# Softcap attention with a maxout feed-forward: two batches loaded as seven tokens per row, and the weights loaded in another order

## Chip, cores, metric

One core of a Trainium2 chip. The time is device microseconds of a whole execution; the profile's span is about 2 us shorter. The runs of one kernel in one call spread over 0.6 to 1.9% here, and a verdict (faster, same, slower by 2%) uses fast runs only, with a 95% interval.

## The reference, cut to what matters

```python
# q, k, v: (8 batches, 12 heads, 448 tokens, 64); cap = 30
scores = cap * tanh(q @ k.T / sqrt(64) / cap)
attn   = softmax(scores)                      # max, exp, sum, division
x      = (attn @ v) -> (8 * 448 tokens, 768)  # heads side by side
out    = maximum(x @ w1, x @ w2) @ w_out      # w1, w2: 768 x 1024, w_out: 1024 x 768
```

## The kernel before

It works through 48 pairs of heads, one an iteration, in groups of three: load q, k, v; cast to bf16; turn q and k (by PE in the first 12 pairs, by DMA later); scores; tanh and exp on ACT; the product with v, which also gives the sums of the softmax; copy to `U`. A group's sums are gathered, inverted, written to DRAM and read back spread over the partitions, and POOL multiplies `U` by them into `x`. The feed-forward matmuls of finished batches fill PE's gaps (`F(n)` takes n of them). As max(a, b) = max(a - b, 0) + b, it uses w1 - w2 and a premultiplied w2 @ w_out.

A tile of 448 tokens is three rows of 128 and 64 more. Before, partition p holds tokens 3p to 3p+2, and the last 64 tokens come separately:

```python
def load(g, what, n0=0, n1=L):            # cut
    nc.sync.dma_start(out=m[:, 2*n0 : 2*n1, :],
        in_=src[b, h0:h1, 0 : NJ*P, :].rearrange("h (p j) d -> p h (j d)", j=NJ))
    ...                                   # the last 64 tokens: one or two more

def transposes(i):                        # pairs 0 to 11
    for j in range(8):
        nc.tensor.transpose(ps[:, j*P : (j+1)*P], kqf[g % 2][:, n, j, :], ident)
    nc.vector.tensor_copy(..., ps)

def invert(g, n0=0, n1=G):
    nc.vector.reciprocal(t[:m, :], sums[g, n0][:m, :])
    nc.sync.dma_start(out=d[:m, :], in_=t[:m, :])          # rec_d <- rec_s
    for h in range(2):                                     # rec_b <- rec_d
        nc.sync.dma_start(out=rb[64*h : 64*h+64, ...], in_=flat[h:h+1].to_broadcast(...))

# in moe(b): the store of 128 tokens of the result, 384 KB
    rows = out[b0*S : b0*S + NJ*P, :].rearrange("(p j) n -> p j n", j=NJ)
    nc.sync.dma_start(out=rows[:, j, :], in_=osb)
```

The buffers in question: `U` (two of 10.5 KB per partition), `osb` (three, for results), and the first `x` buffer, which stages w1 in two halves before it holds an x.

## Time and profile before

| | before |
|---|---|
| time, median of 4 runs | 392.12 us (390.2 to 392.63) |
| PE, ACT, POOL, DVE busy | 92%, 75%, 51%, 42% |
| U copies of pairs 4, 10, 47 on DVE | 44.22, 89.27, 337.94 us |
| stores of 384 KB | 24, median 3.9 us from issue to landing |

I later follow the kernel by the start of each pair's U copy, which DVE does once an iteration (pairs are counted from 0). The last 52 us have no attention left, only feed-forward.

### The profile page before, as it was taken

To read this page: it belongs to the slowest core of one execution; us is meant where nothing else is said; L and a number is where in the kernel's file an instruction comes from. 1 tells how busy PE (TensorE), PEld (TensorE's weight loads), DVE (VectorE), ACT (ScalarE), POOL (GpSimd) and SP (SyncE) were. 2 spreads that over 40 slices of the span, in tenths; PEclk is the share of its full clock that TensorE was granted. 3 is DMA by queue.
4 is the path that set the end of the run, shared out by engine and by line. 5 is a ranking of instruction groups with operands and counts; after the bars stand their busy time and mean duration, and the time that the engine had idled before them with its cause. 6 is when DMAs were issued, how large, how long until landed. Compare 5 with 4: busy or idle time off the path is not lost.

```text
span 390.3 us, 5720 instructions
## 1 busy us (share of the span) xinstructions
PE 358.5 (92%) x2128; PEld 171.8 (44%) x2128; DVE 164.3 (42%) x248; ACT 292.4 (75%) x289; POOL 199.6 (51%) x254
## 2 busy tenths in 40 slices
PE   3468896999999999989998999999999999999995
PEld 1123443544444444434443445444444444455563
DVE  5332657774434533253325433352345333633421
ACT  2699995878899799978998899889998899400000
POOL 4272269674638374656657464729482733651000
PEclk9995998999999999999999999999999999999999
DMA  6998899786779768967989597969796751322022
GB/s 142 280 252 180 242 288 274 198 202 165 149 199 252 198 171 199 260 181 192 217 225 223 142 237 210 255 166 225 219 188 179 166 142 65 90 73 100 23 81 81
DMA packets 106596, 71.50 MB, mean 183 GB/s; under 512 B 61384, under 2 KB 99400, under 8 KB 106568
## 3 DMA queue, kind: packets, MB, share of 16 engines
q1 hardware_dynamic: 104616, 67.99, 67.6%
q0 software_dynamic: 1952, 3.15, 4.6%
q8 instruction: 16, 0.26, 0.3%
q14 instruction: 12, 0.10, 0.1%
HBM read 53.48 MB, written 11.18 MB: 166 GB/s over the span
## 4 chain that ended last, share of the span: by engine, by line
PE 54%; DMA 17%; ACT 7%; SPq 6%; POOL 6%; DVE 5%; issue 3%; POOLq 0%; DVEq 0%; ACTq 0%
PE mm L318 15%; PE mm L333 11%; PE mm L330 9%; PE pv L250 8%; DMA rec_d<-rec_s 7%; DMA rec_b<-rec_d 6%; POOL xT L305 6%; PE s L231 5%; ACT expo L238 3%; ACT tanh L232 3%; DMA vm<-in_v_dram 3%; PE pv L259 2%; SPq L112 2%; SPq L101 1%; DMA xT<-in_moe_w_dram 1%
## 5 line engine op out<-in xcount | busy, mean ns | idle before, releaser
L232 ACT ACTIVATE tanh<-s 128x896 bf16<-128x896 f32 x144 | 126.0, 909 | 36.2 <-PE s L231 35.9
L305 POOL TENSOR_TENSOR xT<-u,rec_b 64x448 bf16<-64x448 f32 x95 | 108.2, 1139 | 86.1 <-DMA rec_b<-rec_d 73.8
L238 ACT ACTIVATE expo<-tanh 128x1792 bf16<-128x1792 bf16 x96 | 144.9, 1510 | 3.0
L265 DVE COPY u<-pv 128x896 f32<-128x896 f32 x48 | 52.3, 1091 | 105.3 <-PE pv L259 80.6
L333 PE MATMUL mm<-wo_sb,gT 128*128 128x384 bf16 x448 | 88.8, 327 | 0.0
L318 PE MATMUL mm<-xT,wd_sb 128*128 128x448 bf16 x384 | 80.8, 353 | 3.3 <-POOL xT L305 1.7
L330 PE MATMUL mm<-wm_sb,xT 128*128 128x384 bf16 x336 | 68.0, 327 | 1.8 <-DVE osb L337 1.8
L250 PE MATMUL pv<-expo,vp 128*128 128x448 bf16 x288 | 66.3, 367 | 1.1 <-ACT expo L238 1.1
L333 PEld LDWEIGHTS <-gT 128*128 128x128 bf16 x448 | 41.9, 98 | 36.5 <-issue 10.8
L337 DVE COPY osb<-mm 128x384 f32<-128x384 f32 x56 | 31.0, 555 | 59.9 <-PE mm L333 54.9
L318 PEld LDWEIGHTS <-wd_sb 128*128 128x128 bf16 x384 | 35.4, 98 | 43.9 <-issue 14.5
L231 PE MATMUL s<-qkT 64*128 64x448 bf16 x288 | 46.0, 370 | 7.7 <-DVE qkT L210 5.2
L322 DVE TENSOR_SCALAR gT<-mm 128x448 bf16<-128x448 f32 x64 | 39.9, 623 | 29.6 <-PE mm L318 28.6
L330 PEld LDWEIGHTS <-xT 128*128 128x128 bf16 x336 | 31.7, 98 | 28.6 <-issue 8.7
L250 PEld LDWEIGHTS <-vp 128*128 128x128 bf16 x288 | 28.2, 101 | 29.1 <-issue 7.7
L132 POOL CAST kqf<-qm 128x1152 bf16<-128x1152 f32 x15 | 17.2, 1147 | 33.9 <-DMA qm<-in_q_dram 33.7
L235 ACT ACTIVATE tanh<-s 128x448 bf16<-128x448 f32 x48 | 26.0, 542 | 4.3 <-PE s L234 4.1
L124 POOL CAST vp<-vm 128x576 bf16<-128x576 f32 x30 | 19.9, 665 | 14.2 <-DMA vm<-in_v_dram 9.4
L132 POOL CAST kqf<-km 128x1152 bf16<-128x1152 f32 x15 | 17.2, 1147 | 12.7 <-DMA km<-in_k_dram 11.9
L231 PEld LDWEIGHTS <-qkT 64*128 64x128 bf16 x288 | 10.9, 96 | 22.8 <-issue 15.1
L209 PE MATMUL mm<-ident,kqf 128*128 128x128 bf16 x96 | 9.8, 248 | 11.5 <-DVE kqf L132 7.7
L186 PE MATMUL mm<-wo_sb,w2T 128*128 128x384 bf16 x96 | 18.7, 328 | 0.0
(44 smaller groups left out, 158.9 us busy)
## 6 DMA issues: line engine op xcount, KB each, us to landing
rec_b<-rec_d SPq DMA_DIRECT2D x30, 336.0 KB, 5.0
out_dram<-osb SPq DMA_DIRECT2D x24, 384.0 KB, 3.9
km<-in_k_dram SPq DMA_DIRECT2D x15, 576.0 KB, 7.0
qm<-in_q_dram SPq DMA_DIRECT2D x15, 576.0 KB, 4.5
vm<-in_v_dram SPq DMA_DIRECT2D x15, 576.0 KB, 4.4
xT<-in_moe_w_dram SPq DMA_DIRECT2D x6, 512.0 KB
wo_sb<-in_moe_w_out_dram POOLq DMA_DIRECT2D x4, 384.0 KB, 7.3
gT<-in_moe_w_dram POOLq DMA_DIRECT2D x6, 256.0 KB, 5.8
```

Source lines behind the costliest of these rows:

```text
L132: eng.tensor_copy(t[:, n0:n1, o : o + NJ, :].rearrange("p n j (h d) -> p n h j d", h=2), m[:, 2 * n0 : 2 * n1, :].rearrange("p (n h) (j d) ...
L231: nc.tensor.matmul(s[:, h, :S], t[r, j * P : (j + 1) * P], qTn[r, :])
L232: nc.scalar.activation(tanh[i][:, 2 * j : 2 * j + 2, :], s[:, :, :S], AF.Tanh, scale=scale / cap)
L238: nc.scalar.activation(expo[i][:, c0:c1, :], tanh[i][:, c0:c1, :], AF.Exp, scale=float(cap))
L250: nc.tensor.matmul(ps[:, h, :S], vp[g % 2][:, n, h, j, :], e[:, 2 * j + h, :], start=(j == 0), stop=False)
L265: nc.vector.tensor_copy(U[g][:, :, n, :], pvt[i][:, :, :S])
L305: eng.tensor_mul(xT[b // 2][r, hp, cs], U[g][r, h, n, :], rec[g, n0][r, n - n0, :])
L318: nc.tensor.matmul(ps[:, :S], wd_sb[:, c, f * P : (f + 1) * P], x[:, c, cs], start=(c == 0), stop=(c == KC - 1))
L322: nc.vector.tensor_relu(g[:, f, cs], ps[:, :S])
L330: nc.tensor.matmul(ps[:, : DM // 2], x[:, c, ts], wm_sb[:, c, hs], start=(c == 0), stop=False)
L333: nc.tensor.matmul(ps[:, : DM // 2], g[:, f, ts], wo_sb[:, f, hs], start=False, stop=(f == FC - 1))
L337: nc.vector.tensor_copy(osb[:, hs], ps[:, : DM // 2])
```

## The change

Intent: fewer and longer packets at the start (1792 B in place of 768 and 256 B), a start in which ACT doesn't wait, weights that are there in time, and no wait for late w1 slices. In the first two batches a partition takes seven consecutive tokens of one head (64 rows a head, two heads for 128 partitions). PE then turns blocks of 64 x 64, and a tile of results holds token 2j of every row in its upper half and token 2j+1 in its lower half, so the store scatters. Cut to the core:

```diff
+    R7 = S // 64
+    def rows(t, b, h0, h1):
+        return t[b, h0:h1, :, :].rearrange("h (r j) d -> (h r) (j d)", j=R7)
     def load(g, what, n0=0, n1=L):
+        if g < NT:                                      # k and q; v has four pieces of its own
+            nc.sync.dma_start(out=t[...], in_=rows(src, b, h0, h1).rearrange("(n p) c -> p n c", p=P))
+            return
     def transposes(i):
-        for j in range(8):
-            nc.tensor.transpose(ps[:, j * P : (j + 1) * P], kqf[g % 2][:, n, j, :], ident)
+        for c, to in todo:                              # 13 blocks
+            for a in range(2):
+                r = slice(64 * a, 64 * a + 64)
+                nc.tensor.transpose(ps[r, to : to + 64], x[r, c : c + D], ident[r, r])
+        nc.tensor.transpose(ps[:, NJ * P : Q0], x[:, NJ * P : Q0], ident)
     def load_w1(c):
-        nc.sync.dma_start(out=w1_in[c % 2], in_=...)
+        w1_in[c] = opool.tile([P, DF], f32, name="osb")
+        nc.sync.dma_start(out=w1_in[c], in_=...)
     def pv_out(i):
+            if g == 0:
+                U[g] = x1.bitcast(f32)...               # the later home of x
     # in moe(b):
-                nc.sync.dma_start(out=rows[:, j, :], in_=osb)
+                if wide: ...                            # later batches, as before
+                else:
+                    o = o.rearrange("(r j) n -> j r n", j=R7)
+                    nc.sync.dma_start(out=o[2 * j : 2 * j + 2, :, :], in_=osb)
     # order: all of w_out and w2 from POOL after the casts of q and k of group 1; w1 from
     # iteration 2; v of group 0 behind q and k of group 1; for groups 0 and 1 the reciprocal
     # early in the iteration and its spread issued by POOL
```

More of the change, by code (lines that the diff above doesn't have):

```diff
@@ L40 @@
     NJ = 3
+    NT = 4
+    R7 = S // 64
     scale = 1.0 / (D ** 0.5)
@@ L69, with flat @@
     qf = [t[:, :, 4:8, :] for t in kqf]
+    def flat(g):
+        return kqf[g % 2].rearrange("p n j c -> p n (j c)")
     ident = const.tile([P, P], bf16, name="ident")
@@ L89, in half, with raw_of @@
         return slice(0, 64) if b % 2 == 0 else slice(64, P)
+    def rows(t, b, h0, h1):
+        return t[b, h0:h1, :, :].rearrange("h (r j) d -> (h r) (j d)", j=R7)
+    def raw_of(g, what):
+        if (g, what) not in raw:
+            raw[g, what] = stage.tile([P, 2 * L * NJ * D + (2 * L if what == "q" else L) * D], f32, name=what + "r")
+        t = raw[g, what]
+        m = t[:, : 2 * L * NJ * D].rearrange("p (h c) -> p h c", c=NJ * D)
+        l = t[:, 2 * L * NJ * D :].rearrange("p (h d) -> p h d", d=D)
+        return t, m, l
     def load(g, what, n0=0, n1=L):
@@ L94, in load @@
         src = {"k": k, "q": q, "v": v}[what]
-        if (g, what) not in raw:
-            raw[g, what] = (
-                stage.tile([P, 2 * L, NJ * D], f32, name=what + "m"),
-                stage.tile([P, 2 * L if what == "q" else L, D], f32, name=what + "l"),
+        t, m, l = raw_of(g, what)
+        if g < NT and what == "v":
+            x = rows(src, b, h0, h1).rearrange("(h r) c -> r h c", r=64)
+            for a in range(2):
+                nc.sync.dma_start(
+                    out=m[64 * a : 64 * a + 64, 2 * n0 : 2 * n1, :], in_=x[:, :, NJ * D * a : NJ * D * (a + 1)]
+                )
+            for par in range(2):
+                nc.sync.dma_start(
+                    out=l[64 * par : 64 * par + 64, n0:n1, :], in_=x[:, par::2, 2 * NJ * D :]
+                )
+            return
+        if g < NT:
+            nc.sync.dma_start(
+                out=t[:, n0 * S : n1 * S].rearrange("p (n c) -> p n c", c=S),
+                in_=rows(src, b, h0, h1).rearrange("(n p) c -> p n c", p=P),
             )
-        m, l = raw[g, what]
+            return
         nc.sync.dma_start(
@@ L119, in cast @@
         b = g * L // NP
-        m, l = raw[g, what]
+        x, m, l = raw_of(g, what)
         if what == "v":
@@ L128, in cast @@
                 eng.tensor_copy(vl[g % 2][r, n0:n1, r], l[r, n0:n1, :])
+            return
+        if g < NT:
+            x = x[:, n0 * S : n1 * S].rearrange("p (n c) -> p n c", c=S)
+            if what == "q":
+                eng.tensor_copy(flat(g)[:, n0:n1, Q0 : Q0 + S], x)
+                return
+            eng.tensor_copy(flat(g)[:, n0:n1, : NJ * P], x[:, :, : NJ * P])
+            for par in range(2):
+                r = slice(64 * par, 64 * par + 64)
+                eng.tensor_copy(kf[g % 2][r, n0:n1, 3, r], x[r, :, NJ * P :])
             return
@@ L148 @@
     x1 = xpool.tile([P, NP, 2 * S], bf16, name="xT").rearrange("p n s -> p (n s)")
-    w1_in = [x1[:, 2 * DF * j : 2 * DF * (j + 1)].bitcast(f32) for j in range(2)]
+    w1_in = {}
     w2b = (
@@ L164, in load_w1 @@
     def load_w1(c):
-        nc.sync.dma_start(out=w1_in[c % 2], in_=moe_w1[c * P : (c + 1) * P, :])
+        w1_in[c] = opool.tile([P, DF], f32, name="osb")
+        nc.sync.dma_start(out=w1_in[c], in_=moe_w1[c * P : (c + 1) * P, :])
     def subtract(c):
-        nc.vector.tensor_sub(wd_sb[:, c, :], w1_in[c % 2], w2b[:, c, :])
+        nc.vector.tensor_sub(wd_sb[:, c, :], w1_in[c], w2b[:, c, :])
     w2T = {}
@@ L207, in transposes @@
         ps = mm_psum.tile([P, 512], f32, name="mm").bitcast(bf16)
-        for j in range(8):
-            nc.tensor.transpose(ps[:, j * P : (j + 1) * P], kqf[g % 2][:, n, j, :], ident)
-        nc.vector.tensor_copy(qkT_of(g)[:, n, :, :].rearrange("p j c -> p (j c)"), ps)
+        x = flat(g)[:, n, :]
+        todo = [(j * D, (j % 3) * P + (j // 3) * 64) for j in range(6)]
+        odd = i // NP % 2
+        todo += [(Q0 + j * D, Q0 + (64 * j if not odd else 0 if j == 6 else 64 + 64 * j)) for j in range(R7)]
+        for c, to in todo:
+            for a in range(2):
+                r = slice(64 * a, 64 * a + 64)
+                nc.tensor.transpose(ps[r, to : to + 64], x[r, c : c + D], ident[r, r])
+        nc.tensor.transpose(ps[:, NJ * P : Q0], x[:, NJ * P : Q0], ident)
+        nc.vector.tensor_copy(qkT_of(g)[:, n, :, :].rearrange("p j c -> p (j c)")[:, : Q0 + S], ps[:, : Q0 + S])
     def cross(g):
@@ L221, in qk @@
         t = qkT[g][:, n, :, :].rearrange("p j c -> p (j c)")
-        o = Q0 + 64 * (i // NP % 2)
+        o = Q0 + (64 * (i // NP % 2) if g >= NT else 0)
         qTn = t[:, o : o + S]
@@ L263, in pv_out @@
         if n == 0:
-            U[g] = upool.tile([P, 2, G, S], f32, name="u")
+            if g == 0:
+                U[g] = x1.bitcast(f32).rearrange("p (h n s) -> p h n s", h=2, n=G)
+            else:
+                U[g] = upool.tile([P, 2, G, S], f32, name="u")
         nc.vector.tensor_copy(U[g][:, :, n, :], pvt[i][:, :, :S])
@@ L278, in gather @@
             )
+    recd = {}
     def invert(g, n0=0, n1=G):
@@ L283, in invert, with spread @@
         nc.vector.reciprocal(t[:m, :], sums[g, n0][:m, :])
-        d = dram.tile([16 * G, 56], f32, name="rec_d")
+        d = recd[g, n0] = dram.tile([16 * G, 56], f32, name="rec_d")
         nc.sync.dma_start(out=d[:m, :], in_=t[:m, :])
+    def spread(g, n0=0, n1=G):
         rb = rec[g, n0] = xpool.tile([P, G, S], f32, name="rec_b")
-        flat = d[:m, :].rearrange("(h n a) c -> h n (a c)", h=2, a=8)
+        lines = recd[g, n0][: 16 * (n1 - n0), :].rearrange("(h n a) c -> h n (a c)", h=2, a=8)
+        eng = nc.gpsimd if g < 2 else nc.sync
         for h in range(2):
-            nc.sync.dma_start(
+            eng.dma_start(
                 out=rb[64 * h : 64 * h + 64, : n1 - n0, :],
-                in_=flat[h : h + 1, :, :].to_broadcast([64, n1 - n0, S]),
+                in_=lines[h : h + 1, :, :].to_broadcast([64, n1 - n0, S]),
             )
@@ L323, in moe @@
         for t in range(3) if b % 2 == 0 else range(3, 7):
-            osb = opool.tile([P, DM], f32, name="osb")
+            osb = opool.tile([P, DF], f32, name="osb")[:, :DM]
             ts = slice(t * P, (t + 1) * P)
@@ L337, in moe @@
                 nc.vector.tensor_copy(osb[:, hs], ps[:, : DM // 2])
+            wide = b * NP >= NT * L
             if t == 3:
                 for n in range(2):
-                    r0 = (b - 1 + n) * S + NJ * P
-                    nc.sync.dma_start(out=out[r0 : r0 + 64, :], in_=osb[64 * n : 64 * n + 64, :])
-            else:
-                b0, j = (b, t) if t < 3 else (b, t - 4)
-                rows = out[b0 * S : b0 * S + NJ * P, :].rearrange("(p j) n -> p j n", j=NJ)
-                nc.sync.dma_start(out=rows[:, j, :], in_=osb)
+                    o = out[(b - 1 + n) * S : (b + n) * S, :]
+                    to = o[NJ * P : S, :] if wide else o.rearrange("(r j) n -> r j n", j=R7)[:, R7 - 1, :]
+                    nc.sync.dma_start(out=to, in_=osb[64 * n : 64 * n + 64, :])
+            else:
+                j = t if t < 3 else t - 4
+                o = out[b * S : (b + 1) * S, :]
+                if wide:
+                    nc.sync.dma_start(out=o[: NJ * P, :].rearrange("(p j) n -> p j n", j=NJ)[:, j, :], in_=osb)
+                else:
+                    o = o.rearrange("(r j) n -> j r n", j=R7)
+                    nc.sync.dma_start(out=o[2 * j : 2 * j + 2, :, :], in_=osb)
     fill_q = []
@@ L358 @@
     NL = N // L
-    NT = 4
     todo = [[] for _ in range(N)]
@@ L365 @@
     for g in range(2, NL):
-        e = 0 if g < NT else 2
-        at(3 * g - 6 - e, load, g, "k")
-        at(3 * g - 5 - e, load, g, "q")
-        at(3 * g - 4, load, g, "v")
-        at(3 * g - (5 if e else 4), cast, nc.gpsimd, g, "k")
-        at(3 * g - (5 if e else 3), cast, nc.gpsimd, g, "q")
-        at(3 * g - 2, cast, nc.gpsimd, g, "v")
-        if g >= NT:
-            at(3 * g - 4, cross, g)
-    at(1, cast, nc.gpsimd, 1, "v")
-    at(0, load_wo, 6)
-    for c in range(KC):
-        at(1 + c, load_w2, c)
-        at(2 + c, load_w1, c)
+        if g < NT:
+            e = 0 if g == 2 else 1
+            at(3 * g - 6 + e, load, g, "k")
+            at(3 * g - 6 + e, load, g, "q")
+            at(3 * g - 5 + e, load, g, "v")
+            at(3 * g - 4, cast, nc.gpsimd, g, "k")
+            at(3 * g - 4, cast, nc.gpsimd, g, "q")
+            at(3 * g - 3, cast, nc.gpsimd, g, "v")
+        else:
+            at(3 * g - 8, load, g, "k")
+            at(3 * g - 7, load, g, "q")
+            at(3 * g - 4, load, g, "v")
+            at(3 * g - 5, cast, nc.gpsimd, g, "k")
+            at(3 * g - 5, cast, nc.gpsimd, g, "q")
+            at(3 * g - 2, cast, nc.gpsimd, g, "v")
+            at(3 * g - 4, cross, g)
+    for c, i in enumerate((2, 2, 3, 4, 5, 6)):
+        todo[i].insert(c if i == 2 else 0, (load_w1, (c,)))
     MS = 3
     fill_const(nc.vector, 0)
-    fill_const(nc.gpsimd, 1)
-    load_wo(0)
-    for n0, n1 in ((0, 1), (1, L)):
-        for what in "kqv":
-            load(0, what, n0, n1)
-    for what in "kqv":
-        load(1, what)
-    for what in "kq":
-        cast(nc.vector, 0, what, 0, 1)
+    load(0, "k", 0, 1)
+    load(0, "q", 0, 1)
+    load(0, "k", 1, L)
+    load(0, "q", 1, L)
+    load(0, "v", 0, 1)
+    load(1, "k")
+    load(1, "q")
+    load(0, "v", 1, L)
+    load(1, "v")
+    cast(nc.vector, 0, "k", 0, 1)
+    cast(nc.gpsimd, 0, "q", 0, 1)
+    fill_const(nc.gpsimd, 1)
     transposes(0)
-    cast(nc.vector, 0, "v", 0, 1)
-    for what in "kqv":
-        cast(nc.vector, 0, what, 1, L)
+    cast(nc.vector, 0, "k", 1, L)
+    cast(nc.vector, 0, "q", 1, L)
     qk(0, 0)
@@ L398 @@
     ex(0, 0, 4)
+    transposes(1)
     qk(0, 2)
@@ L401 @@
     ex(0, 4, 7)
+    cast(nc.vector, 0, "v")
     cast(nc.gpsimd, 1, "k")
-    load_wo(2)
     cast(nc.gpsimd, 1, "q")
-    load_wo(4)
-    transposes(1)
+    for f in range(0, FC, 2):
+        load_wo(f)
+    for c in range(KC):
+        load_w2(c)
+    cast(nc.gpsimd, 1, "v")
     qk(1, 0)
@@ L435 @@
         F(4 if late else 8)
+        first = i < 2 * G + 2
+        if first and i >= G and n == 0:
+            invert(g - 1)
         if i + 1 < N:
@@ L440 @@
             f(*a)
+        if i == G + 1:
+            spread(0)
+        if i == G + 2 or i == 2 * G + 1:
+            normalize(i // G - 1)
         F(6)
@@ L444 @@
         F(6)
+        if i == 2 * G:
+            spread(1)
         if i == N - 1:
             invert(g, 0, G - 1)
-        elif i >= G and n == 0:
+            spread(g, 0, G - 1)
+        elif not first and n == 0:
             invert(g - 1)
-        if i >= G and n == 1:
+            spread(g - 1)
+        if not first and n == 1:
             normalize(g - 1)
@@ L458 @@
     invert(N // G - 1, G - 1, G)
+    spread(N // G - 1, G - 1, G)
     normalize(N // G - 1, 0, G - 1)
```

## The prediction

> **What bounds the kernel now.** I first read the busy time by stretch of the span, because the shares of the whole span (PE 92%, ACT 75%) are averages over stages with different limits. The rows, with PE, PEld, DVE, ACT and POOL busy, the granted clock, the DMA share and the rate:
>
> ```profile
> 0.00:10.00 10.00, 3.12 (x15) 1.16 (x15) 5.29 (x17) 3.12 (x4) 4.38 (x15) 1.00 0.64 147
> 10.00:20.00 10.00, 5.25 (x21) 1.69 (x22) 3.53 (x11) 6.98 (x7) 2.89 (x5) 1.00 1.09 280
> 20.00:30.00 10.00, 6.75 (x44) 3.02 (x41) 3.57 (x4) 9.78 (x11) 7.29 (x13) 0.94 1.14 246
> 30.00:40.00 10.00, 9.09 (x48) 3.66 (x45) 3.60 (x5) 9.87 (x11) 2.45 (x4) 0.54 0.84 175
> ...
> 60.00:70.00 10.00, 7.34 (x47) 3.65 (x47) 8.09 (x10) 5.47 (x7) 9.54 (x14) 0.83 0.86 231
> 70.00:80.00 10.00, 8.93 (x74) 4.87 (x73) 6.85 (x9) 8.00 (x8) 6.59 (x7) 1.00 0.77 200
> ...
> 100.00:120.00 20.00, 20.00 (x124) 9.70 (x122) 6.63 (x10) 18.42 (x19) 9.75 (x14) 1.00 0.89 215
> ```
>
> There are four stages. Until about 20 us the inputs arrive and ACT has gaps. From 20 to 60 us ACT is full (9.3 to 9.9 of 10): tanh and exp of one pair of heads take 3 x 0.909 + 0.542 + 1.697 + 1.323 = 6.3 us by the means of the costliest groups. From 60 to about 90 us nothing is full, with a hole at 60 to 70. After 100 us PE is full nearly to the end. So the change, which edits only the first 85 us or so, can save no more than what PE and ACT lose there; the 300 us behind are a fixed amount of PE work that only starts earlier.
>
> Next the timeline of those stages, with the idle time before an instruction in brackets. Startup, on ACT:
>
> ```profile
> 8.13 1.73 ACT L232 ACTIVATE tanh<-s 128x896 bf16<-128x896 f32 x2 [6.10 <-PE s L231]
> 17.14 1.73 ACT L232 ACTIVATE tanh<-s 128x896 bf16<-128x896 f32 x2 [2.96 <-PE s L231]
> ```
>
> The second hole is pair 1: its scores need the copy of its turned q and k, which DVE makes only after the casts of v, and those wait for v (cast at 14.68). The hole at 60 us:
>
> ```profile
> 52.95 0.59 SPq L165 DMA_DIRECT2D xT<-in_moe_w_dram  x1
> 58.73 2.10 DVE L168 TENSOR_TENSOR wd_sb<-xT,gT 128x1024 bf16<-128x1024 f32 x1 [2.97 <-DMA xT<-in_moe_w_dram]
> 62.35 0.61 PE L209 MATMUL mm<-ident,kqf 128*128 128x128 bf16 x8 [3.13 <-DVE wm_sb L191]
> 64.91 1.73 ACT L232 ACTIVATE tanh<-s 128x896 bf16<-128x896 f32 x2 [4.25 <-PE s L231]
> ```
>
> The third slice of w1 was issued at 52.95 us (its buffer is one of two, and SP had stood waiting for the reciprocals), landed at 58.73, and held DVE, which held the copy that frees PE's accumulator, which held ACT. Last, the marks I measure iterations by, the first weighted-value matmul of pairs 4 and 10:
>
> ```profile
> 41.15 1.43 PE L250 MATMUL pv<-expo,vp 128*128 128x448 bf16 x6
> 87.64 1.30 PE L250 MATMUL pv<-expo,vp 128*128 128x448 bf16 x6
> ```
>
> Six iterations took 46.5 us, 7.7 us each. The stalled one (pair 6 to 7, 54.8 to 65.5) took 10.7, the neighbours 6.6 to 7.1. The chain of work that ended last runs there through a loop of premultiply matmuls, DVE copies, the transposes and DVE again, at some 7.0 us, above ACT's 6.3.
>
> **What the Trainium skill says.** (1) "TensorE: Matmul & The Clock Gate", section "Back-to-back issue gap": about 56 ns per isolated matmul of 128 columns, and an issue floor of about 25 ns at 64 and fewer. The trace agrees at 128: eight transposes take 0.61 us with a mean of 248 ns each, so (610 - 248) / 7 = 52 ns from start to start. It has none of 64 columns. (2) "TensorEngine Tiling (Array Packing)", section "Key Properties": a change of tiling mode drains the array. No number here isolates that. (3) "DMA: Bandwidth & Descriptors", "Specifications": transfers below 512 B lose rate, and the limit of the memory per core is about 358 GB/s. The page of before has 61,384 of 106,596 packets under 512 B, and no slice above 288 GB/s, which agrees in direction. (4) "TensorE: Matmul & The Clock Gate", Part 1: an idle window of about 3.4 us halves the clock. The trace fits: after the 3.13 us wait above, the granted clock of 60 to 70 us is 0.83.
>
> **The change part by part.**
>
> *Seven tokens per row, pairs 0 to 11.* A load of k or q of a group becomes 384 packets of 1792 B in place of 768 of 768 B and 384 of 256 B, and one issue in place of three or two, at about 0.6 us of SP each. Before the first v load, SP issues 4 loads where it issued 5, each twice to four times as useful. Queue 1 now spends 0.676 x 390.3 x 16 / 104,616 = 40 ns of an engine per packet; if some 15 ns of that are fixed (my estimate, not separable here), the 4 x 1536 packets removed are worth 4 x 1536 x 15 / 16 = 5.8 us of the queue, spread over 50 us. That is slack, not path, after 20 us, where ACT is full. v keeps its packets.
>
> In return PE turns each pair by 26 transposes of 64 columns and one of 128 in place of 8 of 128. Before: 8 x 52 = 0.42 us of pace. After, at a floor of 28 ns (a choice between the skill's 25 and half of 56): 26 x 28 + 52 = 0.78 us, and I add 0.15 for two changes of tiling. Extra: about 0.5 us a pair, and I would believe 0.3 to 1.2, because the loads of such small weights might not hide. For pairs 0 to 4 this lies under ACT. For pairs 5 to 11, turned in iterations 3 to 9, it lies in the loop of 7.0 us.
>
> *Order of the start.* The first tanh hardly moves: k lands as now (cast at 3.42), q is cast at the same time by POOL, but 27 cold transposes cost about 1 us more than 8. I leave it at 8.1 us. Pair 1's transposes now come before pair 0's last scores and before the casts of v, so the 2.96 us hole closes. But the matmul that follows in PE's order, the value product of pair 0, still needs all of v of group 0, and v now queues behind k and q of group 1. Bytes ahead of and with it: 15 blocks of 229 KB, 3.44 MB; at an estimated 320 GB/s from 2.2 us it lands near 13 us, the casts are done near 15, the product (2.9 us cold, from 17.33 to 20.24 now) near 18, and the third tanh of pair 1 starts at 18.4 in place of 20.66. Gain carried to pair 4: about 2.3 us, a ceiling too, as ACT's idle time from 8.1 to 60 us is only about 4 us.
>
> *w1 staged in three output buffers, with its first two slices asked for in iteration 2.* SP is no longer blocked by reciprocals there, since the spread of the first two groups is issued by POOL. The 2.97 us wait of DVE goes. *U of the first group in the later home of x* removes the wait of the third group's first U copy for the first normalize. That copy came at 60.76 and the normalize ended at about 58.5, so it alone is worth nothing now, but it would be the next wait behind w1. Together they bring the 10.7 us iteration to an ordinary 7.0, which is 3.7 us.
>
> *w_out and w2 in one go.* The same ten loads on POOL, from about 16 to 23 us (4 x 0.77 + 6 x 0.55 = 6.4 us of POOL), 6.3 MB read. Queue 0 was busy 4.6% of the span, 18 us of all engines, so in one piece they end near 40 us if the other queue takes half. The first w2 block is needed in iteration 3, at about 33 us. This is tight, and I count nothing for it.
>
> Sum: the start -2.3, the hole -3.7, the transposes in six iterations from pair 4 to 10, 6 x 0.5 = +3.0. Net -3.0, so 392.45 - 3.0 = 389.4 us. After pair 10 PE's work is the same as before.
>
> **The rivals.** *A: the small transposes overlap wholly, or the loop of 7.0 us had room for them.* For it: PE is 8.9 busy of 10 at 70 to 80 us, and the 52 ns pace shows that weight loads hide. Against it: the chain that ended last goes through these transposes and the copy behind them. It would keep the 3.0 us: 386 us; with fewer collisions of DVE and POOL 384. *B: the transposes cost over 1 us each, by drains and weight loads.* For it: nothing in the trace; against: the 64-row score matmuls run at 0.48 us for four, so tiles of half the rows do overlap. The loss of 6 to 8 us eats the gain: 392 to 394 us. *C: the one-go weights starve what is needed first* (w2 in iteration 3, group 2, v of group 0). For it: the DMA share is 0.84 to 1.14 from 10 to 60 us already. A new hole of 3 us takes the place of the old one: 392 to 393 us. *D: fewer packets speed up everything early.* ACT is full from 20 to 60 us, so this only lifts the start, which is counted.
>
> **Range and chances.** All losses that the change can reach are about 2.3 + 7 us (PE's idle time in pairs 4 to 10 beyond its work), so faster by over 2% (below 384.6) needs nearly all of them and free transposes; I give it 0.14. Slower by over 2% (above 400.3) needs B or C at more than twice what I think likely: 0.04. The rest is 0.82. Rivals A and B set the range, 384 to 394.
>
> **What would show it right or wrong.** The first value product of pair 4 should start near 39 us, pair 10 near 84.5; no iteration between should be over 8.5 us; the 64-column transposes should take 0.9 to 1.1 us a pair; the subtract should never wait for w1; the third tanh of pair 1 should start near 18.4. It is wrong if v of group 0 lands after 16 us, if PE waits for w2 or w_out, if a group of transposes exceeds 1.5 us, or if PE after 100 us is no longer full.

## The result, and the profile after

The changed kernel takes **421.73 us** (418.18 to 423.19, 4 runs) against 392.12 of before: ratio 1.0751, interval 1.067 to 1.0833. A ratio here is the mean time of one kernel's fast runs over that of the other's of the same rounds, so not quite the ratio of the medians. It is slower by 7.5%, and far outside the predicted range.

Where the time went is seen best by the start of each pair's U copy (us):

| pair | before | after | after - before |
|---|---|---|---|
| 4 | 44.22 | 41.98 | -2.2 |
| 6 | 60.76 | 55.93 | -4.8 |
| 7 | 68.45 | 67.48 | -1.0 |
| 10 | 89.27 | 89.21 | -0.1 |
| 14 | 116.61 | 116.55 | -0.1 |
| 16 | 130.28 | 139.10 | +8.8 |
| 18 | 144.09 | 160.85 | +16.8 |
| 24 | 186.09 | 216.68 | +30.6 |
| 47 | 337.94 | 368.78 | +30.8 |

The stages that the argument was about, up to pair 14, end even. The whole loss comes in jumps after pair 14 (pair 15 is 6.5 us late) and up to pair 24, and nothing is lost after. The chain of work that ended last, of the kernel after, from 100 to 170 us (start, length, what):

```profile
108.16 10.70 DMA rec_d<-rec_s
...
125.93 9.91 DMA vr<-in_v_dram
139.12 10.17 DMA rec_d<-rec_s
```

`rec_d` is the write of a group's reciprocals, 10.5 KB. It takes 10.7 us. The timeline of before, of the SP queue and of POOL:

```profile
107.82 0.55 SPq L345 DMA_DIRECT2D out_dram<-osb  x1
108.47 0.37 SPq L285 DMA_DIRECT2D rec_d<-rec_s  x1
112.55 1.12 SPq L289 DMA_DIRECT2D rec_b<-rec_d  x2
116.44 1.13 POOL L305 TENSOR_TENSOR xT<-u,rec_b 64x448 bf16<-64x448 f32 x1 [3.45 <-DMA rec_b<-rec_d]
```

And of after:

```profile
107.42 0.64 SPq L410 DMA_DIRECT2D out_dram<-osb  x1
108.16 0.82 SPq L341 DMA_DIRECT2D rec_d<-rec_s  x1
119.01 1.14 SPq L348 DMA_DIRECT2D rec_b<-rec_d  x2
123.03 1.12 POOL L364 TENSOR_TENSOR xT<-u,rec_b 64x448 bf16<-64x448 f32 x1 [10.37 <-DMA rec_b<-rec_d]
...
130.37 1.09 DVE L319 COPY u<-pv 128x896 f32<-128x896 f32 x1 [8.48 <-POOL xT L364]
```

Up to the first store the two run 0.1 to 0.4 us apart. Then SP issues the read-back 4.1 us after the write in the one and 10.9 us after it in the other, POOL starts its multiply 6.6 us later, and DVE, whose U buffer POOL must free, stands for 8.5 us. What the DMA engines did meanwhile shows in the busy time by stretch (the last two numbers are the DMA share and the rate). Before:

```profile
113.00:115.00 2.00, 2.00 (x15) 0.86 (x13) 0.56 (x1) 1.59 (x3) 0.00 (x0) 1.00 0.57 177
115.00:117.00 2.00, 2.00 (x14) 0.76 (x12) 0.39 (x1) 1.97 (x3) 0.56 (x1) 1.00 0.89 214
```

After:

```profile
113.00:115.00 2.00, 2.00 (x14) 0.91 (x13) 0.56 (x1) 1.59 (x3) 0.00 (x0) 1.00 0.13 52
115.00:117.00 2.00, 2.00 (x14) 0.78 (x12) 0.45 (x1) 1.97 (x2) 0.00 (x0) 1.00 0.13 52
```

0.13 of 16 engines is two engines, at a steady 52 GB/s; the share stays so from 111 to 118 us (0.09 to 0.14 in windows of 1 us). The store's output view, `o[2*j : 2*j+2, :, :]`, is 2 x 64 x 768: its first dimension is 2. At 52 GB/s its 384 KB (393,216 bytes) take 7.6 us, an estimate that fits these 7 us, against a median of 3.9 us from issue to landing for the stores of before.

The second finding is at 60 us, where the old hole had been. Timeline of after:

```profile
59.95 0.49 DVE L339 RECIPROCAL rec_s<-sums 48x56 f32<-48x56 f32 x1 [2.94 <-DMA sums<-u]
60.91 0.90 PE L259 MATMUL mm<-ident,kqf 64*64 64x64 bf16 x26 [2.57 <-DVE wm_sb L234]
63.96 1.73 ACT L283 ACTIVATE tanh<-s 128x896 bf16<-128x896 f32 x2 [4.17 <-PE s L282]
```

DVE no longer waits for w1. In this profile it waits 2.9 us for the sums of the second group, as the reciprocal now comes early in DVE's order, and PE and ACT wait behind it just as before.

### The profile page after: what moved, and what is told of

Same layout as the page of the kernel before. It is cut to its first block, busy times and chain, and to the rows that moved or that the text cites. A ratio compares the mean times of both kernels' runs of the same rounds, so it can differ in the third digit from the quotient of the medians.

```text
span 421.4 us, 6150 instructions
## 1 busy us (share of the span) xinstructions
PE 366.6 (87%) x2356; PEld 174.1 (41%) x2356; DVE 160.4 (38%) x241; ACT 292.8 (69%) x289; POOL 201.2 (48%) x256
## 4 chain that ended last, share of the span: by engine, by line
PE 51%; DMA 24%; ACT 9%; SPq 6%; POOL 4%; DVE 3%; issue 2%; POOLq 0%; DVEq 0%; ACTq 0%
PE mm L377 13%; PE mm L392 10%; DMA rec_d<-rec_s 9%; PE mm L389 8%; PE pv L301 8%; DMA vr<-in_v_dram 7%; ACT expo L289 5%; DMA rec_b<-rec_d 4%; PE s L282 4%; POOL xT L364 4%; ACT tanh L283 4%; PE mm L229 3%; DMA sums<-u 2%; PE pv L310 2%; SPq L142 2%
## 5 line engine op out<-in xcount | busy, mean ns | idle before, releaser
L364 POOL TENSOR_TENSOR xT<-u,rec_b 64x448 bf16<-64x448 f32 x89 | 101.3, 1138 | 93.9 <-DMA rec_b<-rec_d 90.1
L319 DVE COPY u<-pv 128x896 f32<-128x896 f32 x45 | 49.1, 1091 | 120.8 <-PE pv L310 72.9
L377 PE MATMUL mm<-xT,wd_sb 128*128 128x448 bf16 x384 | 84.8, 366 | 9.2 <-POOL xT L364 8.7
L301 PE MATMUL pv<-expo,vp 128*128 128x448 bf16 x288 | 67.7, 371 | 13.0 <-DVE u L319 8.1
L389 PE MATMUL mm<-wm_sb,xT 128*128 128x384 bf16 x336 | 69.0, 330 | 8.4 <-DVE osb L396 8.4
L377 PEld LDWEIGHTS <-wd_sb 128*128 128x128 bf16 x384 | 36.4, 100 | 52.5 <-issue 25.0
L301 PEld LDWEIGHTS <-vp 128*128 128x128 bf16 x288 | 28.3, 101 | 41.5 <-issue 16.1
L154 POOL CAST vp<-vr 128x576 bf16<-128x576 f32 x30 | 19.9, 662 | 29.3 <-DMA vr<-in_v_dram 25.4
L173 POOL CAST kqf<-qr 128x1152 bf16<-128x1152 f32 x12 | 13.8, 1146 | 23.6 <-DMA qr<-in_q_dram 23.5
L310 PE MATMUL pv<-expo,vl 64*128 64x448 bf16 x96 | 18.1, 373 | 0.0
L285 PE MATMUL s<-qkT 128*128 128x448 bf16 x48 | 17.3, 361 | 0.7 <-ACT tanh L283 0.7
```

The costliest lines, as they stand in the source:

```text
L301: nc.tensor.matmul(ps[:, h, :S], vp[g % 2][:, n, h, j, :], e[:, 2 * j + h, :], start=(j == 0), stop=False)
L319: nc.vector.tensor_copy(U[g][:, :, n, :], pvt[i][:, :, :S])
L364: eng.tensor_mul(xT[b // 2][r, hp, cs], U[g][r, h, n, :], rec[g, n0][r, n - n0, :])
L377: nc.tensor.matmul(ps[:, :S], wd_sb[:, c, f * P : (f + 1) * P], x[:, c, cs], start=(c == 0), stop=(c == KC - 1))
L389: nc.tensor.matmul(ps[:, : DM // 2], x[:, c, ts], wm_sb[:, c, hs], start=(c == 0), stop=False)
```

## Experiments

Two theories of the large loss. **A**: the store with a leading dimension of 2 runs on two DMA engines and holds up everything with a share on them. **B**: something else in the change, the wide stride of the stored rows or the later staging of normalize. The first three kernels ran together.

**Split the store.** The changed kernel, with each store sent as two of 64 rows:

```diff
-                    nc.sync.dma_start(out=o[2 * j : 2 * j + 2, :, :], in_=osb)
+                    for a in range(2):
+                        nc.sync.dma_start(out=o[2 * j + a, :, :], in_=osb[64 * a : 64 * a + 64, :])
```

> The changed kernel with each 128-row output store of the first two batches sent as two stores of 64 rows, the same bytes to the same places. Theory A (the store whose output view begins with a dimension of 2 runs on 2 of the 16 DMA engines, takes about 10 us and holds up the small reciprocal transfers): 386 to 393 us, the DMA share of 110 to 120 us back above 0.6, the reciprocals' write landing in about 4 us in place of 10. Rival B (rows 7 tokens apart are slow to write, or the later staging of normalize is to blame): stays at 415 to 422 us, with the store still taking 7 us or more.

Measured: 394.05 us (391.1 to 395.94, 4 runs), before beside it 394.24 (7 runs); ratio 1.0023, interval 0.9942 to 1.0104. The same bytes go to the same places; all of the loss is gone (to within the interval), and the U copy of pair 24 starts at 184.75. Its timeline:

```profile
105.65 1.20 SPq L411 DMA_DIRECT2D out_dram<-osb  x2
106.95 0.53 SPq L341 DMA_DIRECT2D rec_d<-rec_s  x1
110.61 1.11 SPq L348 DMA_DIRECT2D rec_b<-rec_d  x2
```

The read-back is issued 3.7 us after the write. A holds, B doesn't: the wide stride and the later staging of normalize are both still there.

**The kernel before, on few engines.** Rows, order and addresses of before; only the six stores are cut at 122 + 6 rows (122 = 2 x 61). Cut: the other batches store as before.

```diff
+                if b < 2:
+                    nc.sync.dma_start(out=rows[:122, j, :], in_=osb[:122, :])
+                    nc.sync.dma_start(out=rows[122:, j, :], in_=osb[122:, :])
```

> The kernel before, with the same six stores of the first two batches cut at 122 and 6 rows: 122 has no divisor between 2 and 16 but 2, so if the number of engines is a divisor of the leading count, the big store runs on 2 engines. Nothing else is changed. Theory A: 412 to 425 us, nearly the loss of the changed kernel, with the DMA share near 0.13 after the first store. Rival B: 390 to 394 us, as rows keep the old order.

Measured: 423.39 us (5 runs), ratio 1.0784, interval 1.0719 to 1.0848. Its timeline and its DMA share:

```profile
107.72 0.38 SPq L346 DMA_DIRECT2D out_dram<-osb  x1
...
109.41 0.32 SPq L285 DMA_DIRECT2D rec_d<-rec_s  x1
118.73 1.44 SPq L289 DMA_DIRECT2D rec_b<-rec_d  x2
```

```profile
113.00:115.00 2.00, 2.00 (x15) 0.91 (x13) 0.56 (x1) 1.59 (x2) 0.17 (x1) 1.00 0.13 52
```

So the loss can be put into the kernel before with nothing else of the change: 0.13 and 52 GB/s again, the read-back 9.3 us after the write. Its pairs run like those of the changed kernel: pair 16 at 138.46 (139.10), 18 at 160.90 (160.85), 24 at 217.10 (216.68).

**Four engines.** The same with 124 + 4 rows, with new runs of before. It was run at another time.

> The kernel before with the six stores of the first two batches cut at 124 and 4 rows: 124 divides by 4 and by nothing larger up to 16, so the big store should run on 4 engines. If the time on the store's engines is what hurts, the store takes about half as long as on 2 engines, about 5 us, and most of it fits into the slack of the loop: 393 to 402 us. If having the store in two pieces or having few engines as such hurts, it stays near 420.

Measured: 406.77 us, ratio 1.0339, interval 1.0281 to 1.0397. The big store does run on four engines:

```profile
113.00:115.00 2.00, 2.00 (x14) 0.91 (x13) 0.56 (x1) 1.59 (x2) 1.13 (x2) 1.00 0.25 95
```

The read-back of the first group concerned comes 7.1 us after the write (109.72 to 116.82). The loss is 3.4% with four engines and 7.8% with two: it goes with the time on few engines, not with the store being in two pieces (the split store is in two pieces as well, and loses nothing). I had expected the loop to swallow more of it (up to 402 us).

**From another queue.** Is it the order within SP's queue, or the engines themselves? The changed kernel with the six stores issued by ACT, still of the slow shape:

```diff
-                    nc.sync.dma_start(out=o[2 * j : 2 * j + 2, :, :], in_=osb)
+                    nc.scalar.dma_start(out=o[2 * j : 2 * j + 2, :, :], in_=osb)
```

> The changed kernel with the six slow stores issued from ACT's queue in place of SP's, in the same shape, so still on 2 engines. Theory (on those 2 engines the small reciprocal transfers and the loads stand behind the store in the same queue, as they all come from SP): from another queue they take turns with it, the first reciprocals' write lands in about 4 us in place of 10, and the time falls to 394 to 404 us. Rival (two engines are busy anyway, whichever queue feeds them, or the write itself is what waits): 412 us or more.

Measured: 418.0 us, ratio 1.0586, interval 1.0492 to 1.0679 (the record's verdict is "unclear", and three of the 11 runs of before beside it were slow; the interval, of fast runs, lies above 2%). Timeline:

```profile
107.07 1.15 ACTq L410 DMA_DIRECT2D out_dram<-osb  x1
...
107.47 0.53 SPq L341 DMA_DIRECT2D rec_d<-rec_s  x1
...
112.63 1.12 SPq L348 DMA_DIRECT2D rec_b<-rec_d  x2
```

The first reciprocals' write is through in 5.2 us in place of 10.9, as the theory had it, so part of that delay was the order in one queue. But the total is the rival's (412 us or more), not mine (394 to 404). Two things mix in it and I have not parted them. The next transfers share the two engines too: POOL's first multiply waited 5.5 us for its reciprocals. And ACT, which now issues the stores between its own activations, once stood idle for 9.0 us, until it had issued one (at 130.64). So that the engines alone would cost as much stays open.

**The smaller question: where did the expected 3 us go?** The start reached pair 6 with a lead of 4.8 us; the early reciprocal lost most of it at pair 7. The third kernel puts that reciprocal back late (stores split):

```diff
-        if first and i >= G and n == 0:
-            invert(g - 1)
+        if i == G:
+            invert(0)
...
         if i == 2 * G:
+            invert(1)
             spread(1)
```

> As the first run, but the reciprocal of the second group is put back to late in iteration 6, behind PE's transposes of that iteration, where the kernel before has it. Theory: the expected 3 us at the hole near 60 us were lost because the reciprocal, put early in DVE's order, waits 2.9 us for its sums and holds the copies that PE needs; then this run is 2 to 3.5 us faster than the first, and no iteration from pair 4 to 8 takes over 8 us. Rival: the transfers of that time are simply late (a queue of weights), so another instruction waits in its place: within 1 us of the first run.

Measured: 391.77 us (4 runs, one of them slow), ratio 0.9948, interval 0.9871 to 1.0025; the split-store kernel beside it 1.0023, so the 2 to 3.5 us are not clear of noise. No iteration from pair 4 to 8 was over 7.2 us. But in the split-store kernel none was over 7.7: that profile has no wait for the sums, and pair 7 starts at 63.07 (before 68.45). So the wait at 60 us in the changed kernel's profile was a transfer that came late in that run, not a fixed cost of the early reciprocal. Up to 60 us the changed kernel and the split-store one are the same program, so this is a difference between executions.

In both kernels the lead at pair 8 (5.2 us with the stores split, 4.7 with the late reciprocal) is then cut: 3.6 and 1.6 us are left at pair 9, 1.9 and 1.5 at pair 10. Timeline of the split-store kernel:

```profile
78.74 1.09 DVE L319 COPY u<-pv 128x896 f32<-128x896 f32 x1 [2.21 <-POOL xT L364]
...
80.35 0.60 PE L259 MATMUL mm<-ident,kqf 64*64 64x64 bf16 x26 [1.56 <-DVE wm_sb L234]
...
83.61 1.73 ACT L283 ACTIVATE tanh<-s 128x896 bf16<-128x896 f32 x2 [3.38 <-PE s L282]
```

The fourth group's first U copy (pair 9) waits 2.2 us for POOL to finish the second normalize, in both kernels, and PE and ACT wait behind it. The kernel that is early meets a U buffer that is not yet free. I tried this in two ways; a third U buffer doesn't fit into memory.

*Half of the first two normalizes on DVE* (on top of the late reciprocal):

```diff
-            normalize(i // G - 1)
+            normalize(i // G - 1, 0, G, nc.vector)
```

> The third run (split stores, late reciprocal), with half of the first two normalizes given to DVE, which takes 0.62 us for what POOL takes 1.14. Theory: the lead of that kernel at pair 9 (1.6 us here, 3.6 in the first run) is lost at pair 10 because the fourth group's first U copy waits for POOL's second normalize; with 3.4 us less of POOL work that wait goes, pair 10 starts its U copy at 84 us or earlier in place of 87.8, and the end is 386 to 389 us if the lead lasts. Rival: the lead at pair 10 is lost again in the loop behind it, where the waits for normalize do not depend on it: pair 10 earlier, the end within 1 us of that run.

Measured: 409.04 us (6 runs, two of them slow), ratio 1.0344, interval 1.0285 to 1.0404: wrong in both theories. Its waits of DVE and of PE (total, times, longest):

```profile
DVE xT L364 <- DMA rec_b<-rec_d: 14.8, 3, 5.3
```

```profile
PE mm L259 <- DVE wm_sb L234: 15.7, 2, 8.3
```

The reciprocals come late. POOL can wait for them, but DVE also frees PE's accumulators, so DVE's wait became PE's. The multiplies took 1.24 us each there besides (three in 3.72 us), not the 0.62 that I had from a single one at the end.

*The second normalize ahead of the casts that stand before it on POOL* (on top of the split stores):

```diff
+        if i == 2 * G + 1:
+            normalize(1)
         for f, a in todo[i]:
             f(*a)
-        if i == G + 2 or i == 2 * G + 1:
-            normalize(i // G - 1)
+        if i == G + 2:
+            normalize(0)
```

> The first run (split stores), with POOL's second normalize ahead of the casts of the fifth group in iteration 7. Theory: the U copy of pair 9 waited 2.2 us for that normalize, which began 4.5 us late behind those casts; now it waits for nothing, pair 10's U copy starts at 84 to 85.5 us in place of 87.4, and if a lead lasts in the loop the end is 1.5 to 3 us below that run, 389 to 392 us. Rival: the wait is for the spread's transfer, or the casts being later holds the transposes of the fifth group: pair 10 not before 87 us, or the lead gone by pair 13.

Measured: 392.34 us (6 runs) beside 395.35 of before (11 runs): ratio 0.9932, interval 0.9873 to 0.9991. It is the fastest of all by its ratio, though only 0.7%. The rival was right about the mechanism:

```profile
72.46 8.01 POOL L364 TENSOR_TENSOR xT<-u,rec_b 64x448 bf16<-64x448 f32 x6 [3.70 <-DMA rec_b<-rec_d]
```

POOL now waits 3.7 us for the spread, DVE still waits 1.0 us for POOL, pair 10 starts at 87.55 (87.37 in the split-store run), and at pair 13 it is at 110.47, behind the 110.02 of before. So the wait for U became shorter and pair 10 came no earlier; no run removed that wait.

**w1 alone.** The kernel before with w1 staged in the output buffers and asked for from iteration 2 (the `load_w1` hunk of the change and the new order of its calls, nothing else; U of the first group stays where it was):

> The kernel before with one part of the change: w1 staged in the three output buffers and asked for from iteration 2 on. Theory (the hole of 10.7 us between pairs 6 and 7 came from the late w1, but closing it only moves the wait to the U buffers and the normalizes): the hole falls to 7 to 8 us, DVE no longer waits for w1, but the first U copy of the third or fourth group waits for POOL, and the whole is within 1% of before. The prediction's step (the hole is worth 3.7 us of the end): 388 to 389 us.

Measured: 392.76 us (6 runs), ratio 0.9999, interval 0.9946 to 1.0052. The long iteration of before (10.6 us for pair 6 by the U copies, 50.19 to 60.76) is not gone but becomes 9.5 us for pair 6 and 7.2 for pair 7 (50.22, 59.71, 66.94); the lead is 1.5 us at pair 7 and 0.9 at pair 10, and at pair 47 the kernel is 0.65 us behind. DVE no longer waits for w1, but the third group's first U copy does for POOL:

```profile
59.71 1.09 DVE L266 COPY u<-pv 128x896 f32<-128x896 f32 x1 [2.21 <-POOL xT L306]
```

The prediction had named this as the next wait behind w1, and the full change removes it by the new home of U. So this run shows that w1 alone is worth nothing; it doesn't test the two together. My theory had the whole right, and the hole too small (7 to 8 us).

**The rows undone.** The changed kernel with only the rows taken back (loads, casts, transposes, stores as before), the new order kept. The edit is that of the change in reverse for those four places.

> The changed kernel with only the seven tokens per row undone (rows, casts, transposes and stores as before), all of its new order kept. Theory: the loss of 29 us is all in the store that came with the rows, so this run is at 389 to 394 us; and as the rows save packets in the start, pair 4 comes 1 to 2 us later than in the first run. Rival: part of the loss is in the new order (one-go weights, the spread on POOL): 396 us or more.

Measured: 403.12 us, ratio 1.0243, interval 1.0185 to 1.0301 (unclear at 2%, but clear of 1). The rival holds: the new order alone is a loss. The profile loses it at the start: pair 4 starts at 50.38 (before 44.22, split-store kernel 41.50), because a reciprocal waits 4.1 us for its sums, PE's scores wait 5.5 us behind it, and v of a group lands late (POOL's cast waits 6.1 us for it).

```profile
45.08 0.49 DVE L332 RECIPROCAL rec_s<-sums 48x56 f32<-48x56 f32 x1 [4.08 <-DMA sums<-xT]
...
46.77 0.93 PE L275 MATMUL s<-qkT 64*128 64x448 bf16 x4 [5.53 <-DVE qkT L254]
```

So, between these two profiles, the rows are worth some 9 us to that order at pair 4, far more than the slack I had called them, and the order cannot be judged without them.

## Why the prediction was wrong

1. **The step that failed**: "So the change, which edits only the first 85 us or so, can save no more than what PE and ACT lose there; the 300 us behind are a fixed amount of PE work that only starts earlier", and its repetition "After pair 10 PE's work is the same as before". The diff also changes the store of the first two batches, whose six issues run from 107.4 to 194.0 us in the profile after, and that store had no line in my sum. It cost about 30 us. The work of PE was indeed the same; the waits were not, and neither was the clock. From 100 to 225 us PE is busy for 122.6 us before and 101.7 after, so my own sign of being wrong, PE no longer full after 100 us, came true. And in that stretch the granted clock is 1.00 throughout before, while after it is 0.5 for 6.8 us each from 128.7, 159.4 and 214.0 us: over the whole run PE is busy for 366.6 us in place of 358.5, of which the new transposes are under 2 us (8.5 + 2.9 in place of 9.8).
2. The cause is shown both ways: taken out of the changed kernel (1.0023) and put into the one before (1.0784, against 1.0751). The rule was at hand: the Trainium skill, "DMA: Bandwidth & Descriptors", section "Rules for kernel authors", says under "Use all 16 engines" that the slowest dimension sets the number of engines, and that an outermost dimension of fewer than 16 confines the whole DMA to at most that many. Traces agree: a share of 0.13 with a dimension of 2. The cuts at 122 and 124 rows are above 16, so that limit does not reach them; they rested on the assumption that the number is a divisor of the rows, and the shares of 0.13 (122 = 2 x 61) and 0.25 (124 = 4 x 31) fit it. I read that page for packet sizes, and read the store's new view only for its addresses.
3. None of my rivals held it either. C, a transfer that starves what is needed, was nearest, but I looked for it among the weights before 60 us.
4. **The transposes**: expected 0.9 to 1.1 us a pair, of which 0.93 was the pace of my sum. Measured is 0.60 us from the first transpose to the next other matmul (44.63 to 45.23), against 0.45 before (52.44 to 52.88); besides, the first transpose now starts 0.26 us after the matmul ahead of it, before 0.16. So the extra is 0.24 us a pair, not 0.5, and the term of +3.0 us about 1.5. The single starts in the trace show which part was mis-sized. The 26 come in pairs, one on each of two disjoint tiles of the array, 3 to 4 ns apart, and most pairs start 28 or 29 ns after the last, so all 26 start within 0.40 us and not in 26 x 28 ns = 0.73 us. The 0.15 us for two changes of tiling was near: some 0.09 on the way in (0.256 us from start to start in place of 0.162) and 0.10 on the way out (0.125 in place of 0.03). (The 52 ns that I read for 128 columns are 55 to 56 by the single starts; my mean of 248 ns mixed two clocks.) The result lies between my sum and rival A. Timeline of after:

```profile
44.63 0.60 PE L259 MATMUL mm<-ident,kqf 64*64 64x64 bf16 x26
45.16 0.23 PE L260 MATMUL mm<-ident,kqf 128*128 128x128 bf16 x1
```

5. **The start**: the first tanh came earlier than I thought, at 6.79 us and not 8.1. The third of pair 1 came later, at 19.74 and not 18.4, since v of group 0 was cast from 15.73 on, where I had it land near 13: the page of after has 251 and 275 GB/s in the first 21 us, not the 320 that I had estimated. The value product of pair 4 started at 40.03 (expected near 39, before 41.15). Right in direction, about half the size.
6. **The hole, -3.7 us**: DVE doesn't wait for w1 any more, as predicted, and with the stores mended no iteration from pair 4 to 8 is over 7.7 us. But the closed hole did not shorten the end: a lead of 5.2 us at pair 8 is 1.9 at pair 10 and 0.4 at pair 47. At pair 9 a wait of 2.2 us for U takes part of it (seen in two profiles; no run removed it). The prediction had read that "nothing is full" from 60 to 90 us; its own line has POOL, which frees U, busy for 9.54 of 10 us from 60 to 70. What took the rest in the loop is not settled. PE's waits there, from 1 to 2 us for a normalize, fall differently in every profile, and the times of one kernel spread over 4 us or more. Some of that spread is the clock at the end: from the U copy of pair 47 to the end of the span the profile of before takes 52.4 us and that of the split-store kernel 56.5, with a granted clock of 0.5 for 6.8 us from 352.0 in the second and 1.00 there in the first. So a lead of a few us is read better from the starts than from one run's total.
7. **Fewer packets**: called slack with no place in the path after 20 us. The run with the rows undone points the other way: in the new order, which asks for all weights at once, pair 4 comes at 50.4 without the rows and at 41.5 with them. Whether it is the packets, the larger number of issues of SP or the transposes is not parted, and the 15 ns per packet that I had assumed was measured by no run. My sum of parts treated rows and order as independent, and they aren't.

What the change intended, with a store that is not held to two engines, is worth between nothing and 1% (ratios 1.0023, 0.9948 and 0.9932 in three variants, of which only the last has an interval below 1), near the 389.4 us that I predicted for the whole; that doesn't make the prediction right, as the kernel given was another.

## What to carry to other kernels

When a change alters a layout, follow it to the last transfer that leaves the chip, and look at each DMA's first dimension on both sides: 128 rows sent as 2 x 64 can be worse than two transfers of 64 (7.5% slower than before here, against 0.2%). A DMA share that stands still at a simple fraction (2/16, 4/16) while small transfers take 7 to 11 us is the sign to look for. And a hole closed early in a kernel is worth what is left of it at the end, so compare the starts of the same piece of work all along the span before counting it.

## What the Trainium skill lacked or had wrong

- "TensorEngine Tiling (Array Packing)", section "Key Properties", says that a change of tiling mode drains the array, without a size. Where the work here goes from 128 x 128 to 64 x 64, the gap from start to start is 0.09 us longer, and where it goes back 0.10 us (point 4 on why the prediction was wrong has the starts); that this is the drain alone was not isolated.
- "DMA: Bandwidth & Descriptors" gives the rule for the number of engines but no figure for what a transfer on few engines does to others: a write of 10.5 KB from the same queue took 10.9 us in place of 4.1 until its read-back could be issued, and six such stores cost the kernel before 7.8% on 2 engines and 3.4% on 4.
- The same page, "Rules for kernel authors", advises one 128-partition transfer in place of two on disjoint halves. Where the one is written with a leading dimension of 2, the two halves are better: a ratio to before of 1.0023 against 1.0751 (394.05 and 421.73 us).
